# A gated linear attention with a rational feed-forward on one core: pairs of heads joined in one matmul step, fourteen joined polynomial steps, and another order of all steps

## The chip, the core and the metric

The kernel runs on one core of a Trainium2 chip. The core has five engines with queues of their own: TensorE (PE in the profile, with its weight loads as PEld), VectorE (DVE), ScalarE (ACT), GpSimd (POOL) and SyncE (SP, which here only issues transfers). Each engine executes its own instructions in the order in which the program lists them; between engines, semaphores make one wait for another. Transfers run on 16 DMA engines that all queues share. The metric is the device time of one execution in microseconds; the kernel before took 212.11 us as the median of 3 runs (211.64 to 213.5).

## The reference

Two stages. The first is a recurrence per batch (4) and head (8) over 768 positions, with head size 48; the second is a feed-forward layer on 3072 tokens of width 384 with 2048 hidden units and a rational function between its two products.

```python
f = 1.0 / (1.0 + np.exp(-f_logit))
for t in range(S):
    state = f[:, :, t, :, None] * state + einsum('bhd,bhde', k[:, :, t], v[:, :, t])
    y[:, :, t] = einsum('bhd,bhde->bhe', q[:, :, t], state)
...
h = x @ w_in
P = a[0] + a[1]*h + a[2]*h**2 + a[3]*h**3
Q = 1 + abs(b[0])*abs(h) + abs(b[1])*h**2
return (P / (Q + 1e-6)) @ w_out
```

## The kernel before

**Units.** The work is cut into 12 units of 256 tokens: 4 batches times 3 stretches of the sequence (units 0 to 3 are the first stretches, 8 to 11 the last ones, and a unit needs the state of the unit four before it). The 256 tokens are interleaved in two (i), and a unit has two blocks (j) of 128 tokens, each on 64 partitions. Eight heads make four pairs (a).

**Steps of the recurrence.** `ld` loads f, k, q (issued by SP) and v (issued by POOL). `ef` and `ls` (ACT) make the logarithm of the gate, `cs` (PE) sums it along time, `A` (ACT) exponentiates it, once for k (x=1) and once for q (x=0). `xa` (DVE or POOL, a `p` in the step) multiplies k and q with it. `T` transposes the result on PE, `Te` copies it out of PSUM (ACT with an `s`, else DVE). `sc` multiplies k and q into scores, for two pairs of heads at a time (g), `mk` (DVE) masks them. `yb` multiplies the masked scores with v, `yi` multiplies q with the state before the block. `vm` copies the columns of v that lie across a boundary. `ic` and `si` (PE) and `st` (DVE) make the next state. `ye` (ACT with `s`, else DVE) copies y to x, in bf16.

**The step `yb`** holds, for both i, four pieces of two heads, the pairs a0 to a1, and both j. Each matmul is a small one: 64 partitions in (the block j), 32 columns out (the pair a), 128 columns of scores. A matmul thus occupies one of eight tiles of the PE array, two row groups by four column groups. In the kernel before, every unit has two such steps, one for pairs 0 and 1 and one for pairs 2 and 3, of 32 matmuls each, with other steps between them in nine of the twelve units.

**Steps of the feed-forward.** `h` (PE) is the first product, four tiles of 128 hidden units at a time; `hy` (ACT) copies it out. Then follow on 8 or 16 hidden tiles at a time (2048 or 4096 columns): `sq` (DVE) or `sa` (ACT) the square, `ab` (DVE) the absolute value, `zd` (a transfer that adds, issued by POOL) or `zv` (DVE) the sum for Q, `rq` (ACT) the reciprocal, `p1` and `p2` (DVE, one multiply and one add by a scalar) the two halves of the polynomial, `pm` (DVE) a product, `ta` (a transfer that adds) or `tv` (DVE) their sum, and `gm` (DVE) P/Q. `o` (PE) is the second product, four hidden tiles of one block at a time; `oe` copies it out and `so` stores it. `tab` loads an activation table on ACT.

**What sets the order.** `ORDER` (lines 19 to 100) is a written list of all steps. The program takes them one by one (the loop at the end of the kernel function), so the list gives each engine's order of instructions and each queue's order of transfers. `@n` is the slot of PSUM (four slots of two banks) that a step fills: it waits until the earlier content of that slot has been read. `!m` sets a mark and `^m` holds a POOL step behind the marked one. Rings of buffers add waits too: there is one ring place for the transposed q and k (`T`) and one for the masked scores (`scm`), two for `A`, three for the loads, three for g and z, two for the square.

In the loop at the end, each step is made as
```python
made = steps[name](*(int(x.lstrip("@")) if x.lstrip("@").isdigit() else x for x in args))
```

Of the kernel before, what the change touches and what calls it, by code (L numbers as in the profile page):

```python
# [8 lines left out]
F32 = mybir.dt.float32  # L9
BF16 = mybir.dt.bfloat16  # L10
# [18 lines left out]
hy 0 8 12; fb; ld 4 f; yb 1 0 2 @3; hy 0 12 16; yb 1 2 4; xa 2 1; yi 1 1; ye 1 s; p1 0 8 16; T 2 @2  # L29
A 3 1; ab 0 8 16; h 1 12 16 @1; Te 2 s; sq 0 8 16; h 1 8 12 @3; p2 0 8 16; hy 1 12 16; pm 0 8 16 !m3; ld 3 q  # L30
ic 2 @0; hy 1 8 12; vm 2 ^m3; sc 2 1 @2; st 2 0; sc 2 0 @1; mk 2 1; ld 3 k; si 2 1; ef 5; h 0 0 4 @3; st 2 1
ls 5; ld 6 f; ab 1 8 16; h 0 4 8 @2; ef 4; tv 0 8 16 !m5; hy 0 0 4; ld 4 k; xa 3 0 2 4 p ^m5; h 1 4 8 @0
mk 2 0; ls 4; ld 4 q; ld 3 v ^m4; hy 0 4 8; h 1 0 4 @3; xa 3 1; ld 4 v; hy 1 4 8; xa 3 0 0 2; yb 2 0 2 @1
ld 7 f; zv 0 8 16; hy 1 0 4; T 3 @2; p1 0 0 8; ef 6; yi 2 1; yb 2 2 4; sq 1 0 8; Te 3 s; cs 4 @0; ld 8 f
ye 2 s; ab 1 0 8; sc 3 0 @3; cs 5 @2; A 4 0; ab 0 0 8 !m8; xa 4 0 2 4 p ^m8; mk 3 0; A 4 1; ic 3 @1; sa 1 8 16
h 2 8 12 @0; st 3 0; ld 5 k; sq 0 0 8; si 3 1; h 2 12 16 @3; hy 2 8 12; pm 0 0 8 !m7; zd 0 0 8; ld 5 q
xa 4 1 2 4 p ^m7; ls 6; sc 3 1 @0; st 3 1 !m6; A 5 1; ld 6 k; vm 3 ^m6; mk 3 1; h 2 4 8 @1; ld 5 v; hy 2 12 16
xa 4 1 0 2; ef 7; yi 3 1 @0; xa 4 0 0 2; yb 3 0 2; wo 12 16; p1 1 8 16; hy 2 4 8; T 4 @3; wo 8 12
pm 1 8 16 !m10; A 5 0; ic 4 @1; wo 4 8; xa 5 1 0 2 p ^m10; si 4 0; Te 4 s; yb 3 2 4; st 4 0 !m11; ye 3 !m9
# [69 lines left out]
def kernel(  # L109
# [135 lines left out]
    def const_z(i):  # L245
# [375 lines left out]
```

## Time and profile before

| | |
|---|---|
| median of 3 runs | 212.11 us |
| the profiled execution, its own time | 210.19 us |
| its span, first to last instruction | 208.5 us |
| granted TensorE clock, mean | 0.988 |
| PE busy | 191.0 us, 92% |
| DVE busy | 187.0 us, 90% |
| ACT busy | 186.1 us, 89% |
| POOL busy | 77.8 us, 37% |
| from HBM and to HBM | 25.17 MB and 4.72 MB |

The busy time of an engine is the time in which at least one of its instructions is under way; instructions of one engine overlap a little, so the time from one start to the next is shorter than a duration. The windows of the profile give busy time by stage, with the number of instructions behind an x. In the timeline, square brackets hold the idle time of the engine ahead of an instruction and what ended it. The chain of waits is followed back from the end.

### The profile page before, as it was taken

Reading aid. Unit: us, or ns where it says so; the run is one execution under the profiler, and the core shown is the slowest. Engines: PE = TensorE matmul, PEld = TensorE weight load, DVE = VectorE, ACT = ScalarE, POOL = GpSimd, SP = SyncE. Lnnn points to the kernel's source line nnn. Section 1 sums busy time; section 2 is a strip of 40 time slices with the busy share of each in tenths; the row PEclk is TensorE's granted clock in tenths of the full one; section 3 lists DMA queues with packets and bytes.
Section 4 is the critical chain, followed back from the end, with each engine's and each line's share of the span. In section 5 each row is a group of like instructions: output and inputs, shape, how many; then the busy total and the mean of one; then the engine's idle time right before and its main releaser. Section 6 shows DMA issues by size and latency. Waiting matters only on the chain.

```text
span 208.5 us, 6605 instructions
## 1 busy us (share of the span) xinstructions
PE 191.0 (92%) x2894; PEld 139.4 (67%) x2894; DVE 187.0 (90%) x235; ACT 186.1 (89%) x172; POOL 77.8 (37%) x99
## 2 busy tenths in 40 slices
PE   1297799989999999999999999999999999999991
PEld 1165487867767778766888677678766766776650
DVE  3378579999999999999999989999999999999970
ACT  4756389999999999999999999999999999999871
POOL 6060610516961535026151760641674433412000
PEclk9999699999999999999999999999999999999998
DMA  6999999799999499999999999899999999998955
GB/s 98 287 300 186 271 220 253 186 220 233 168 206 202 85 176 152 249 267 265 208 222 252 250 199 229 209 200 210 185 191 163 214 211 195 193 190 183 238 146 167
DMA packets 61820, 43.15 MB, mean 207 GB/s; under 512 B 51424, under 2 KB 56544, under 8 KB 61792
## 3 DMA queue, kind: packets, MB, share of 16 engines
q0 software_dynamic: 20528, 23.86, 69.3%
q1 hardware_dynamic: 41184, 18.78, 34.7%
q8 instruction: 22, 0.36, 0.6%
q10 hardware_dynamic: 80, 0.10, 0.2%
q14 instruction: 6, 0.05, 0.1%
HBM read 25.17 MB, written 4.72 MB: 143 GB/s over the span
## 4 chain that ended last, share of the span: by engine, by line
PE 75%; DVE 10%; DMA 6%; SPq 4%; issue 2%; ACT 1%; DVEq 0%
PE op L549 31%; PE hp L469 26%; PE y L389 6%; SPq L209 4%; PE cs L304 3%; DMA v<-in_v_dram 3%; PE tp L345 3%; PE sc L368 2%; DMA q<-in_q_dram 2%; DVE scm L376 2%; DVE g L528 2%; PE sv L434 2%; DVE state L459 1%; PE sv L444 1%; DVE qkp L331 1%
## 5 line engine op out<-in xcount | busy, mean ns | idle before, releaser
L549 PE MATMUL op<-w_out_sb,g 128*128 128x384 bf16 x384 | 68.6, 326 | 0.0
L469 PE MATMUL hp<-x,w_in_sb 128*128 128x256 bf16 x576 | 68.0, 273 | 0.3 <-DVE state L459 0.3
L469 PEld LDWEIGHTS <-w_in_sb 128*128 128x128 bf16 x576 | 55.4, 98 | 9.4 <-issue 0.7
L549 PEld LDWEIGHTS <-g 128*128 128x128 bf16 x384 | 35.8, 98 | 22.6 <-DVE g L540 0.4
L481 ACT CAST hy<-hp 128x1024 bf16<-128x1024 f32 x48 | 47.8, 1027 | 2.6 <-PE hp L469 2.3
L508 ACT ACTIVATE z<-z 128x4096 bf16<-128x4096 bf16 (+1 forms) x16 | 44.5, 2780 | 1.1 <-DVE z L499 1.1
L540 DVE TENSOR_TENSOR g<-g,z 128x2048 bf16<-128x2048 bf16 (+2 forms) x24 | 28.9, 1218 | 1.1 <-issue 0.6
L503 POOL DMA_DIRECT2D z<-h x20 | 20.6, 1077 | 24.7 <-ACT h L490 17.0
L528 DVE TENSOR_TENSOR g<-g,h 128x2048 bf16<-128x2048 bf16 (+1 forms) x21 | 28.8, 1373 | 0.1
L376 DVE TENSOR_TENSOR scm<-sc,mask 128x1024 bf16<-128x1024 f32 x24 | 28.8, 1216 | 0.0
L490 ACT ACTIVATE h<-hy 128x2048 bf16<-128x2048 bf16 (+1 forms) x13 | 26.8, 2073 | 0.0
L326 ACT ACTIVATE A<-cs 128x768 f32<-128x768 f32 (+3 forms) x26 | 19.0, 779 | 6.5 <-PE cs L312 6.5
L532 POOL DMA_DIRECT2D g<-hy x15 | 13.8, 943 | 28.3 <-DVE g L528 9.3
L304 PE MATMUL cs<-lsp,Ui 128*128 128x384 bf16 (+1 forms) x39 | 12.0, 371 | 10.1 <-ACT lsp L294 8.7
L518 DVE TENSOR_SCALAR g<-hy,a_sb 128x2048 bf16<-128x2048 bf16 (+1 forms) x23 | 18.9, 829 | 1.4 <-ACT hy L481 1.4
L331 POOL TENSOR_TENSOR qkp<-k,A 128x384 bf16<-128x384 f32 x11 | 11.0, 1025 | 23.6 <-DVE g L540 10.4
L523 DVE TENSOR_SCALAR hy<-hy,a_sb 128x2048 bf16<-128x2048 bf16 (+1 forms) x20 | 18.3, 915 | 0.4
L209 POOL DMA_DIRECT2D v<-in_v_dram x12 | 12.1, 1012 | 15.7 <-DVE qkp L331 8.3
L494 DVE TENSOR_SCALAR z<-hy 128x2048 uint16<-128x2048 uint16 (+1 forms) x21 | 15.8, 764 | 0.0
L459 DVE TENSOR_TENSOR state<-sv,A 128x384 bf16<-128x384 f32 x20 | 11.0, 552 | 4.5 <-PE sv L444 2.4
L389 PE MATMUL y<-scm,v 64*32 64x128 bf16 x384 | 14.0, 218 | 0.8 <-DVE scm L376 0.7
L331 POOL TENSOR_TENSOR qkp<-q,A 128x384 bf16<-128x384 f32 x10 | 10.0, 1010 | 11.5 <-ACT A L326 5.5
(70 smaller groups left out, 246.4 us busy)
## 6 DMA issues: line engine op xcount, KB each, us to landing
z<-h POOLq DMA_DIRECT2D x20, 512.0 KB, 7.5
g<-hy POOLq DMA_DIRECT2D x15, 512.0 KB, 7.8
f<-in_f_logit_dram SPq DMA_DIRECT2D x11, 384.0 KB, 5.8
k<-in_k_dram SPq DMA_DIRECT2D x11, 384.0 KB, 7.7
q<-in_q_dram SPq DMA_DIRECT2D x11, 384.0 KB, 7.8
v<-in_v_dram POOLq DMA_DIRECT2D x12, 192.0 KB, 7.7
out_dram<-f SPq DMA_DIRECT2D x12, 192.0 KB, 3.9
out_dram<-osb SPq DMA_DIRECT2D x10, 192.0 KB, 6.4
```

Source lines behind the costliest of these rows:

```text
L209: return eng.dma_start(out=s[what][:, hh].rearrange("p h i d -> p h (i d)"), in_=src[s["b"], hh, t0:t0 + NT, :].rearrange("h (p i) d -> p ...
L331: i = (nc.gpsimd if eng == "p" else nc.vector).tensor_mul(s["qk"][:, x, :, hh, 0:D], s["qk"[x]][:, hh].rearrange("p h i d -> p i h d"), s[ ...
L376: return nc.vector.tensor_mul(t, s["sc", g].rearrange("s r a i t -> s (r a) (i t)"), mb)
L389: nc.tensor.matmul(s["y"][32 * a:32 * a + 32, j, kk * C:kk * C + C].rearrange("e (i t) -> e i t", i=2), lhsT, rhs, start=(j, a) not in s[" ...
L469: nc.tensor.matmul(t[:, m - m0, :].rearrange("f (j t) -> f j t", j=UB), w_in_sb[:, kk, m * P:(m + 1) * P], s["x"][:, :, kk, :], start=(kk ...
L481: nc.scalar.copy(fl(big(s, "hy"), m0, m1), fl(s["hp", m0], 0, m1 - m0))
L490: return nc.scalar.activation(fl(big(s, "h2"), m0, m1), fl(big(s, "hy"), m0, m1), AF.Square)
L503: return nc.gpsimd.dma_start(out=fl(big(s, "z"), m0, m1), in_=fl(big(s, "h2"), m0, m1), accum_op=ALU.add)
L508: return nc.scalar.add_instruction(mybir.InstActivation(name=nc.get_next_instruction_name(), func=AF.Reciprocal, ins=[nc.scalar.lower_ap(f ...
L528: return nc.vector.tensor_mul(fl(big(s, "g"), m0, m1), fl(big(s, "g"), m0, m1), fl(big(s, "h2"), m0, m1))
L540: return nc.vector.tensor_mul(fl(big(s, "g"), m0, m1), fl(big(s, "g"), m0, m1), fl(big(s, "z"), m0, m1))
L549: nc.tensor.matmul(s["op", g][:, j, 0:DM], big(s, "g")[:, m, C * j:C * j + C], w_out_sb[:, m, :], start=(s["on", j] == 1), stop=(s["on", j ...
```

## The change

1. `yb` is called once per unit, for all four pairs (12 steps of 64 matmuls where there were 24 of 32). The function is the same; the four pairs are the inner loop, so that eight matmuls that follow one another go to the eight different tiles.
2. Seven more `p1` and two more `p2` cover 16 hidden tiles at once; with those that did so before, 14 of the two kinds are joined. Three more `gm` and two more `pm` are joined too.
3. Some work moves between engines: one half of a `sq` goes from DVE to ACT (as `sa`, of which two more are joined), two `ye` go from ACT to DVE, one `oe` of half a unit from ACT to DVE, and one half of a q product (`xa`) from DVE to POOL.
4. `T` can be cut (a `c` in the step): 64 transposes of 64 by 64 in place of 16 of 128 by 128, with another layout of the result. Units 7, 10 and 11 use it.
5. A new step `dm` multiplies zeros by zeros (two matmuls of 512 columns each, whose result nobody reads); it stands in the list twice. `cz 4` clears its operand.
6. The list has another order from the first step to the last, on all engines and queues.

The core of the diff (the list of steps is shown at its first and last lines):

```diff
-cu 1; cz 1; ld 0 f 2 4; ld 0 v; ab_ b s; cz 3; cz 0; ld 0 f 0 2; ci; ld 0 q 2 4; ld 1 f; cu 0; ld 0 k 0 2
-ef 0 2 4; ls 0 2 4; cm; ld 0 k 2 4; cz 2; fa; cs 0 2 4 @0; ef 0 0 2; ls 0 0 2; ld 0 q 0 2; cs 0 0 2 @1; ld 1 k
-A 0 1 0 2; A 0 1 2 4; A 0 0 2 4; A 0 0 0 2; fr; ld 2 f; ef 1; xa 0 1 2 4; ls 1; xa 0 0 2 4; vm 0 v; cs 1 @2
-xa 0 0 0 2; ld 1 q; xa 0 1 0 2 !m0; ld 1 v ^m0; ld 3 f; ic 0 @3; wi 2 8 16; A 1 1; wi 3 8 16; A 1 0
-T 0 0 2 @0; st 0 0; ld 2 q; ab_ a s; wi 1 8 16; xa 1 1 2 4; T 0 2 4 @1; wi 0 8 16; Te 0 0 2 s; sc 0 0 @2
-xa 1 0 0 2; Te 0 2 4 s; xa 1 0 2 4; ef 2; si 0 1; sc 0 1 @0; xa 1 1 0 2; st 0 1; T 1 @1; mk 0 0; ld 2 k
-mk 0 1; yb 0 0 2 @3; yi 0 1; Te 1; ef 3; yb 0 2 4; ic 1 @2; ls 2; st 1 0 !m1; sc 1 1 @0; ld 2 v ^m1; ye 0 s
-cs 2 @1; mk 1 1 !m4; ls 3; sc 1 0 @3; wi 0 0 8; A 2 0; si 1 1; ld 5 f; cs 3 @0; wi 3 0 8; st 1 1; A 2 1
-vm 1 v !m2; wi 2 0 8; mk 1 0; xa 2 0 0 2 p ^m2; A 3 0; h 0 8 12 @2; wi 1 0 8; xa 2 0 2 4; h 0 12 16 @1
...
-so 8 0 2; o 10 0 4 8; gm 11 12 16; o 10 0 0 4; rq 11 0 8; gm 11 8 12; o 11 1 12 16 @2; tv 11 0 8
-o 11 0 8 12 @1; oe 9 0 2 s; o 11 0 12 16; gm 11 0 4; oe 10 0 2 s; o 11 1 8 12; so 9 0 2; gm 11 4 8; o 11 0 0 4
-o 11 0 4 8; so 10 0 2; o 11 1 4 8; oe 11 0 1 s; o 11 1 0 4; so 11 0 1; oe 11 1 2 s; so 11 1 2
+cu 1; cz 0; ld 0 k 2 4; cu 0; ld 0 f 2 4; cz 3; ld 1 f; ci; ld 0 f 0 2; cm; ab_ b s; ld 0 v; cz 2; cz 1
+ld 0 q 0 2; ld 0 k 0 2; ld 0 q 2 4; ef 1; ef 0 2 4; ld 1 q; ls 0 2 4; ef 0 0 2; cs 0 2 4 @0; fa; ls 0 0 2
+ls 1; cs 0 0 2 @1; ld 1 k; vm 0 v; fr; cs 1 @2; A 0 1 2 4; A 0 1 0 2; A 0 0 0 2; xa 0 1 0 2; A 0 0 2 4; ld 2 f
+xa 0 1 2 4; A 1 0; xa 0 0 0 2 !m0; ld 1 v ^m0; T 0 0 2 @3; ld 3 f; ic 0 @1; wi 2 8 16; Te 0 0 2 s; wi 0 8 16
+A 1 1; ld 2 k; ab_ a s; st 0 0; wi 3 8 16; xa 0 0 2 4; wi 1 8 16; xa 1 0 2 4; T 0 2 4 @0; xa 1 1 0 2
+xa 1 0 0 2; sc 0 0 @3; Te 0 2 4 s; xa 1 1 2 4; ld 2 q; ef 2; si 0 1; cz 4; sc 0 1 @2; st 0 1; ls 2; T 1 @0
+mk 0 1; ef 3; mk 0 0; ls 3; yi 0 1 @1; ic 1 @2; Te 1 !m1; yb 0 0 4; ld 2 v ^m1; ye 0 s; st 1 0; sc 1 1 @3
+vm 1 v; si 1 1; mk 1 1; sc 1 0 @0; wi 3 0 8; cs 3 @1; ld 5 f; wi 2 0 8; mk 1 0; cs 2 @3; wi 0 0 8; A 3 1
+wi 1 0 8; st 1 1; h 0 8 12 @0; A 2 1; A 3 0; xa 2 1 0 2; h 0 12 16 @2; xa 2 1 2 4; A 2 0; ld 4 f; fb
+hy 0 8 12; yb 1 0 4 @1; hy 0 12 16; yi 1 1; xa 2 0; ic 2 @3; ye 1; sa 0 8 16; T 2 @0; st 2 0; h 1 8 12 @2
...
+o 10 0 4 8; gm 11 12 16; rq 11 0 8; so 8 0 2; o 10 0 0 4; p2 11 0 8; o 11 0 12 16 @0; gm 11 8 12
+o 11 1 12 16 @1; tv 11 0 8; oe 9 0 2 s; o 11 0 8 12; so 9 0 2; oe 10 0 2 s; o 11 1 8 12; gm 11 0 4; gm 11 4 8
+o 11 0 0 4; so 10 0 2; o 11 0 4 8; o 11 1 4 8; oe 11 0 1 v; o 11 1 0 4; so 11 0 1; oe 11 1 2 s; so 11 1 2
...
+    zz = consts.tile([P, 512], BF16, name="zz")
...
+        elif i == 4:
+            return nc.vector.memset(zz, 0.0)
...
     def T(n, *args):
-        s = unit(n)
-        a0, a1, sl = args if len(args) == 3 else (0, HP, args[0])
-        t = s["tp", a0] = slot(sl, [P, 2, 2, HP, P], BF16, "tp")
+        s = unit(n)
+        *ab, sl = [x for x in args if x != "c"]
+        a0, a1 = ab or (0, HP)
+        cut = "c" in args
+        t = s["tp", a0] = slot(sl, [P] + ([UB, 2, 2, HP, R] if cut else [2, 2, HP, P]), BF16, "tp")
         for x in (1, 0):
             for i in range(2):
                 for p in range(a0, a1):
-                    nc.tensor.transpose(t[:, x, i, p, :],
-                                        s["qk"][:, x, i, 2 * p:2 * p + 2, :].rearrange("t h d -> t (h d)"), ident)
+                    if cut:
+                        for j in range(UB):
+                            m = slice(R * j, R * j + R)
+                            for par in range(2):
+                                nc.tensor.transpose(t[E * par:E * par + E, j, x, i, p, :],
+                                                    s["qk"][m, x, i, 2 * p + par, :], ident[m, m])
+                    else:
+                        nc.tensor.transpose(t[:, x, i, p, :],
+                                            s["qk"][:, x, i, 2 * p:2 * p + 2, :].rearrange("t h d -> t (h d)"), ident)
...
+    def dm(i, sl):
+
+        t = slot(sl, [P, 2, 512], F32, "dm")
+        for b in range(2):
+            nc.tensor.matmul(t[:, b, :], zz[:, 0:P], zz, start=True, stop=True)
```

`Te`, `sc` and `yi` read the cut layout through a view with the block j outermost; their instructions keep their number and sizes.

More of the change, by code (lines that the diff above doesn't have):

```diff
@@ L30 @@
[L30 to L39, printed above, removed]
@@ new lines @@
+ld 11 q; ta 3 0 8; ab 5 0 8; sc 7 1 @2; hy 6 4 8; zd 4 0 8; ld 9 v; sq 5 8 16 !m21; h 6 12 16 @0
+xa 9 0 2 4 p ^m21; mk 7 1; h 6 8 12 @3; tab 1; rq 3 0 8; p2 4 0 8; yi 7 0 @2; yi 7 1; zv 4 8 16; yb 7 0 4
+ta 4 0 8; ic 8; ye 7 s; ta 4 8 16; ld 10 v ^m19; st 8 0; hy 6 12 16; tv 3 8 16; h 7 4 8 @2; zd 5 0 8
+hy 6 8 12; p1 5 0 16; T 8 @1; rq 3 8 16; h 7 0 4 @0; pm 5 8 16; ld 10 k; Te 8 s; h 7 8 12 @3; gm 3 0 8
+hy 7 4 8; vm 8 v; cs 10 @1; gm 3 8 16; hy 7 0 4; o 3 0 4 8 @2; pm 5 0 8; hy 7 8 12; o 3 0 12 16; rq 4 0 16
@@ L352, in Te @@
         s["T"] = ring["T"][n % len(ring["T"])]
-        dst, src = (t[:, :, :, a0:a1].rearrange("p x i a t -> p (x i) (a t)") for t in (s["T"], s["tp", a0]))
+        if len(s["tp", a0].shape) == 6:
+            s["T"] = s["T"].rearrange("p x i a (j t) -> p (x i a j t)", j=UB).rearrange(
+                "p (j x i a t) -> p j x i a t", j=UB, x=2, i=2, a=HP)
+            dst, src = (t[:, :, :, :, a0:a1].rearrange("p j x i a t -> p (j x i) (a t)") for t in (s["T"], s["tp", a0]))
+            s["Tj"] = [s["T"][:, j] for j in range(UB)]
+        else:
+            dst, src = (t[:, :, :, a0:a1].rearrange("p x i a t -> p (x i) (a t)") for t in (s["T"], s["tp", a0]))
+            s["Tj"] = [s["T"][:, :, :, :, R * j:R * j + R] for j in range(UB)]
         if "s" in args:
@@ L402, in yi @@
             for a in range(HP):
-                ymm(s, j, a, kk, state(s, j)[:, a, 32 * kk:32 * kk + 32], s["T"][:, 0, :, a, R * j:R * j + R])
+                ymm(s, j, a, kk, state(s, j)[:, a, 32 * kk:32 * kk + 32], s["Tj"][j][:, 0, :, a, :])
     def yb(n, a0=0, a1=HP, sl=None):
```

121 lines of the change are left out of this document (61 added, 60 removed).

## The prediction

> **What bounds the kernel now.** I read the page first, for the balance of the engines, then three windows of it.
>
> ```profile
> PE 191.0 (92%) x2894; PEld 139.4 (67%) x2894; DVE 187.0 (90%) x235; ACT 186.1 (89%) x172; POOL 77.8 (37%) x99
> PE   1297799989999999999999999999999999999991
> DVE  3378579999999999999999989999999999999970
> ACT  4756389999999999999999999999999999999871
> ```
>
> ```profile
> 0.00:30.00 30.00, 18.66 (x372) 14.22 (x373) 17.30 (x50) 17.48 (x26) 10.51 (x24) 0.94 1.12 226
> 30.00:200.00 170.00, 168.21 (x2502) 122.93 (x2500) 167.93 (x184) 166.15 (x144) 67.29 (x75) 1.00 1.06 207
> 200.00:208.50 8.50, 4.14 (x26) 2.25 (x24) 1.74 (x3) 2.43 (x5) 0.00 (x0) 0.90 0.50 139
> ```
>
> The columns after the length are the busy times of PE, PEld, DVE, ACT and POOL, then the clock and the DMA. From 30 to 200 us three engines are full at once: DVE is idle for 170 - 167.93 = 2.07 us, ACT for 3.85, PE for 1.79. What is lost lies ahead of 30 us (DVE 12.7, ACT 12.5) and behind 200. So a faster PE alone would gain nothing that DVE and ACT do not also give. Now the chain of waits (start, length, what), for PE's own rates.
>
> ```profile
> 109.31 1.68 PE y L389 x88
> ...
> 115.02 0.89 PE tp L345 x16
> 115.91 2.60 PE op L549 x16
> ...
> 123.38 1.33 PE hp L469 x12
> 124.71 1.27 PE y L389 x88
> ...
> 158.26 0.56 PE y L389 x32
> ...
> 185.91 18.24 PE op L549 x112
> ```
>
> The last row is PE at work without a gap up to 204.15 us. The other two engines end just ahead of it (timeline):
>
> ```profile
> 198.14 1.91 ACT L508 ACTIVATE z<-z 128x2048 bf16<-128x2048 bf16 x1 [1.06 <-DVE z L499]
> 200.55 1.29 DVE L540 TENSOR_TENSOR g<-g,z 128x1024 bf16<-128x1024 bf16 x2
> ```
>
> The last `gm` ends at 201.84, and PE works 2.31 us more. Behind it, in both lists, stand 12 `o` matmuls whose cost is 2.60 / 16 = 0.163, 1.95 us. So DVE has 0.36 us of slack at the end; all three engines are the bound.
>
> **The change on DVE.** Groups of instructions, with mean ns after the busy time:
>
> ```profile
> L518 DVE TENSOR_SCALAR g<-hy,a_sb 128x2048 bf16<-128x2048 bf16 x22 | 17.6, 805 | 1.4 <-ACT hy L481 1.4
> L518 DVE TENSOR_SCALAR g<-hy,a_sb 128x4096 bf16<-128x4096 bf16 x1 | 1.3, 1343 | 0.0
> L523 DVE TENSOR_SCALAR hy<-hy,a_sb 128x2048 bf16<-128x2048 bf16 x16 | 12.9, 809 | 0.3
> L523 DVE TENSOR_SCALAR hy<-hy,a_sb 128x4096 bf16<-128x4096 bf16 x4 | 5.4, 1338 | 0.1
> L540 DVE TENSOR_TENSOR g<-g,z 128x2048 bf16<-128x2048 bf16 x18 | 21.7, 1216 | 0.3 <-ACT z L508 0.2
> L540 DVE TENSOR_TENSOR g<-g,z 128x4096 bf16<-128x4096 bf16 x2 | 4.6, 2288 | 0.6 <-issue 0.6
> L485 DVE TENSOR_TENSOR h<-hy 128x2048 bf16<-128x2048 bf16 x10 | 12.2, 1220 | 0.0
> L454 DVE TENSOR_SCALAR x<-y,sig 128x768 bf16<-128x768 f32 x2 | 2.0, 1013 | 0.0
> L331 DVE TENSOR_TENSOR qkp<-q,A 128x384 bf16<-128x384 f32 x12 | 6.5, 551 | 0.4 <-DMA q<-in_q_dram 0.4
> ```
>
> Seven more joined `p1` save 7 x (2 x 0.805 - 1.343) = 1.87; two `p2` 2 x (2 x 0.809 - 1.338) = 0.56; three `gm` 0.43; two `pm`, taken at the rows of `gm`, 0.29. One `sq` that goes saves 1.22, one half `xa` 0.55; two `ye` cost 2.03. Together -2.89 by durations. But starts lie closer than durations say:
>
> ```profile
> 29.86 0.81 DVE L518 TENSOR_SCALAR g<-hy,a_sb 128x2048 bf16<-128x2048 bf16 x1 [1.40 <-ACT hy L481]
> 30.59 0.69 DVE L494 TENSOR_SCALAR z<-hy 128x2048 uint16<-128x2048 uint16 x1
> ```
>
> The next one starts 0.73 us after the first, so 0.08 of each instruction is covered by its neighbour. 14 instructions fewer lose 14 x 0.08 = 1.12 of that cover: **DVE -1.8 us**. The `oe` on DVE comes behind the last `gm`, where DVE is free. `cz 4` falls into the start.
>
> **On ACT.** Its rows:
>
> ```profile
> L490 ACT ACTIVATE h<-hy 128x2048 bf16<-128x2048 bf16 x12 | 23.1, 1940 | 0.0
> L490 ACT ACTIVATE h<-hy 128x4096 bf16<-128x4096 bf16 x1 | 3.7, 3658 | 0.0
> L452 ACT ACTIVATE x<-y 128x768 bf16<-128x768 f32 x10 | 8.1, 809 | 2.5 <-PE y L389 2.4
> ```
>
> `sa` goes from 12 halves and 1 whole to 9 and 3: +1.49. Two `ye` go: -1.62. With three instructions fewer, at the same overlap, **ACT +0.1 us**. Of its 3.85 us of idle time after 30 us most waits for PE (`hy`, `ye`) or for `zv` at the end; with PE ahead I let 1.5 us of it go, between 0 and 3.85.
>
> **On PE.** A unit with two separate `yb` takes 1.68 us with its `yi` (88 matmuls); one in which the two stood together (unit 8) 1.27. How eight tiles run is seen there, in PE's timeline:
>
> ```profile
> 124.93 0.33 PE L389 MATMUL y<-scm,vmp 64*32 64x128 bf16 x16
> 125.04 0.33 PE L389 MATMUL y<-scm,v 64*32 64x128 bf16 x12
> ```
>
> While the two halves ran into each other, 16 matmuls started in 0.11 us, 6.9 ns each. A half alone has four tiles, and its row of 32 is 0.56 us, 17.5 ns each. I take a joined `yb` at 64 x 6.9 ns plus 0.12 for filling and draining (an estimate), 0.56 us; the other bound is two halves' worth, 1.12, no gain. In nine units that saves 0.56; in the three where the halves stood together, which are 1.68 - 1.27 = 0.41 shorter already, 0.15. Together 5.5 us, some 4 of them in the full stretch. A cut `T` has 64 matmuls in four tiles: between 0.44 and 1.12 us (the same two rates) against 0.89, near 0.6 I think, since its moving side has 64 columns and not 128; three save 0.9 (between 1.3 saved and 0.7 lost). A `dm` costs two matmuls of 512 columns, by the slope between `hp` (256 columns, 0.111) and `op` (384, 0.163) 0.215 each: 0.43 twice, the first in the start, where PE idles. So **PE -4.5 us** in the full stretch (from +1 to -6), more than the others give, and PE stops being the tightest. What that costs: a joined `yb` waits for the second `mk` of its unit, and all of PE's queue behind it.
>
> ```profile
> L376 DVE TENSOR_TENSOR scm<-sc,mask 128x1024 bf16<-128x1024 f32 x24 | 28.8, 1216 | 0.0
> ```
>
> In the new list at least 3 us of `h` and `o` stand between the last `sc` and the `yb` of each unit from 2 on (unit 7: two `h` at 1.33 and two `yi`; unit 11: two `o` at 0.65, one `h`, two `yi`), against one `mk` of 1.22 or two. I count the wait as nothing; without that cover it is up to 1.2 us a unit.
>
> **The start.** Rows of PE, DVE and ACT, then the chain:
>
> ```profile
> 3.42 0.52 ACT L289 ACTIVATE f<-f 128x384 f32<-128x384 f32 x1 [1.32 <-DMA f<-in_f_logit_dram]
> 10.05 0.56 DVE L331 TENSOR_TENSOR qkp<-k,A 128x384 bf16<-128x384 f32 x1 [3.42 <-DMA k<-in_k_dram]
> 22.19 0.32 PE L304 MATMUL cs<-lsp,Ui 128*128 128x384 bf16 x1 [1.36 <-issue]
> 24.66 0.56 DVE L459 TENSOR_TENSOR state<-sv,A 128x384 bf16<-128x384 f32 x1 [2.45 <-PE sv L444]
> 26.14 2.65 PE hp L469 x24
> ```
>
> ```profile
> GB/s 98 287 300 186 271 220 253 186 220 233 168 206 202 85 176 152 249 267 265 208 222 252 250 199 229 209 200 210 185 191 163 214 211 195 193 190 183 238 146 167
> ```
>
> Before, f comes first and k last: ACT begins at 3.42, DVE then waits 3.42 us for k. After, SP issues half of k, half of f, all of f of unit 1 and only then the other half of f, and ACT's first step is `ef 1`. That needs 768 KB; at 98 to 287 GB/s (5.2 us slices) some 4 us, so ACT begins near 5.7, 2.3 us later. In return `ls 1` is done ahead of the first `A`, k is there when `A` is, and `xa` begins near 10.5 (5.7, then two whole and four half steps and two `A`, at the 0.52 of a half), half a microsecond later than before. POOL issues v behind the constants and not between them; `ic` needs it only after `xa`, which I count as time enough. POOL also gets one more half `xa` over the whole kernel, at a share of 37%: nothing. Then the new list has `sc 1 0` ahead of both `cs` of units 2 and 3. Before, PE sat 1.36 us for nothing that the profile shows, then did a `cs`, and `sc 1 0` came after it: the 2.45 us of DVE. With `mk 1 0` right behind `mk 1 1` these go, and `cs`, `A`, `h` and `hy` follow earlier. Against it: `st 0 0` (0.56) and its wait for `ic` ahead of the last `xa` of unit 0, and `cz 4`. I take **-2.0 us** for the start, for DVE as for ACT; the ends are -3.9 (the waits of 2.45 and 1.40 both gone) and +2.3 (ACT's late beginning never made good).
>
> **The sum.** DVE: -1.8 - 2.0 - 0.3 of end slack = -4.1. ACT: +0.1 - 2.0 - 1.5 = -3.4. PE: -4.5 and its earlier start. The smallest gain decides, ACT's, -3.4, shortened to -3.3 for the `dm` in mid-stretch: span 205.2, with the 1.69 us around it 206.9 against 210.19. The median stands 1.92 above that execution, so it should come to 212.11 - 3.3 = **208.8 us**, 1.6% faster. About 1% is what a measurement of this kernel tells from no change.
>
> **Rivals.** (a) The three engines interlock as before but the start gains nothing, because the late f costs ACT what the earlier `sc` gives: -1.5, 210.6. For it: the 768 KB ahead of the first ACT step. Against: DVE's 3.42 us of waiting for k is room for it.
>
> (b) The joined `yb` does not do what it says, the eight tiles running no faster than four: PE stays the bound at its old work plus 0.43 and up to 0.7, only the start is gained: -1, 211. Against it: the 16 matmuls in 0.11 us.
>
> (c) Slower: PE's instructions do not arrive in time. Instructions too are fetched by DMA:
>
> ```profile
> q8 instruction: 22, 0.36, 0.6%
> ```
>
> That is 16 KB a packet. The gap of 1.36 us came after 223 matmuls and as many weight loads, at a place where no engine was late. The change uses up instructions faster: 128 in 0.56 us for a `yb`, and the three cut `T` add 288. If such a gap opens at six of the twelve units, 8.2 us are lost against 3.3 gained: 217. It decides against the change from four gaps on (5.4 - 3.3 = 2.1, 1%). Against it: the full stretch of before has no such gap, though 88 matmuls pass in 1.27 us there.
>
> [...]
>
> (d) ACT's and DVE's idle time goes wholly as PE runs ahead: -6, 206.
>
> **Chances.** Forecast (207.3 to 210) 0.49, (d) 0.11: faster by over 1% 0.60. (a) 0.16 and (b) 0.07: within 1%, 0.23. (c), with `yb` held by late masks as its smaller kin, 0.17. The range runs from (d), with the most that the start gives, 204.6, up through (a) and (b) to the first part of (c), 214.0.
>
> **What would show it.** Joined `yb` rows of 64 near 0.56 us; DVE busy near 184.5 and ACT near 186; the first `h` near 24.5 us and not 26; no gap of PE named "issue" over 1 us; more PE idle time than 1.79 us between 30 us and the end. It is wrong if PE shows gaps between 60 and 180 us, or if `xa` of unit 0 begins after 12 us.

## The result, and the profile after

The changed kernel takes 212.36 us (median of 12 runs, 210.24 to 213.23), the kernel before beside it 210.34 us (12 runs, 208.09 to 213.5): a ratio of 1.013, 95% interval 1.0089 to 1.017. It is 1.3% slower, where 1.6% faster was forecast. The profiled execution of the changed kernel took 210.24 us and is the fastest of its twelve; that of before, 210.19 us, is near the middle of its own. So the two profiles show what the change did at its best, and not what it costs in most executions. Ratios leave out executions over 1.5% slower than the fastest of the same kernel, medians keep them; the kernel with only `yb` joined, below, has no ratio, since four of its six were such.

The profile's page of the changed kernel, then its busy times in the same three windows as before (length, PE, PEld, DVE, ACT, POOL, clock, DMA):

```profile
PE 188.6 (90%) x3042; PEld 135.6 (65%) x3042; DVE 188.7 (90%) x223; ACT 186.0 (89%) x168; POOL 80.7 (39%) x100
...
q8 instruction: 24, 0.39, 0.7%
```

```profile
0.00:30.00 30.00, 19.56 (x394) 14.66 (x395) 18.84 (x52) 18.70 (x27) 9.49 (x23) 1.00 1.10 215
30.00:200.00 170.00, 164.93 (x2629) 118.81 (x2627) 167.44 (x169) 166.03 (x140) 71.18 (x77) 1.00 1.07 209
200.00:209.00 9.00, 4.16 (x25) 2.09 (x23) 2.38 (x4) 1.30 (x3) 0.00 (x0) 0.99 0.50 133
```

TensorE did 3.3 us less in the full stretch and now idles 5.07 us there; VectorE and ScalarE idle 2.56 and 3.97 us, as before (2.07 and 3.85). VectorE has 12 instructions fewer and 1.7 us more busy time. The chain of waits shows the joined `yb`, the cut `T`, and TensorE twice without work that it waited for:

```profile
21.46 0.14 DVE vmp L400
21.60 0.86 issue
22.46 0.34 PE sv L461
...
27.67 0.61 PE y L406 x58
28.29 0.29 issue
28.58 0.53 PE y L406 x18
...
76.64 0.67 PE y L406 x64
97.33 0.64 PE tp L352 x64
125.68 1.11 PE y L406 x88
```

A joined `yb` takes 0.67 us (forecast 0.56, two halves 1.12), with its `yi` 1.11 where it was 1.68 or 1.27; a cut `T` 0.64 against 0.89.

Now VectorE and GpSimd side by side, in the timeline (start, length, what). Line 546 is `p2`, 393 `mk`, 471 `ye`, 559 `tv`, 331 `xa`:

```profile
49.00 1.22 DVE L393 TENSOR_TENSOR scm<-sc,mask 128x1024 bf16<-128x1024 f32 x1
50.13 1.39 DVE L546 TENSOR_SCALAR hy<-hy,a_sb 128x2048 bf16<-128x2048 bf16 x1
51.45 1.41 DVE L541 TENSOR_SCALAR g<-hy,a_sb 128x4096 bf16<-128x4096 bf16 x1
52.77 1.00 DVE L471 TENSOR_SCALAR x<-y,sig 128x768 bf16<-128x768 f32 x1
53.70 1.53 DVE L559 TENSOR_TENSOR g<-g,hy 128x2048 bf16<-128x2048 bf16 x1
...
111.14 1.45 DVE L546 TENSOR_SCALAR hy<-hy,a_sb 128x2048 bf16<-128x2048 bf16 x1
```

```profile
49.28 1.40 POOL L331 TENSOR_TENSOR qkp<-k,A 128x384 bf16<-128x384 f32 x1
...
52.99 1.14 POOL L331 TENSOR_TENSOR qkp<-k,A 128x384 bf16<-128x384 f32 x1
...
110.54 1.49 POOL L331 TENSOR_TENSOR qkp<-q,A 128x384 bf16<-128x384 f32 x1
```

A half `p2` took 0.809 us before; these two take 1.39 and 1.45, and the `tv` 1.53 where its like take 1.22. Each began while a GpSimd product was still under way. `mk` and `ye` beside the same products keep their 1.22 and 1.00. Seven VectorE instructions are longer than the shortest of their shape by over 0.1 us (0.15 to 0.65 each), 2.7 us together; all seven lie beside GpSimd's products, its copies (`vm`) or its transfer issues. Before, none is: nearly the whole of each GpSimd product lies beside a `mk`, `ye` or `st` (18.2 of 21.4 us beside `mk` alone). One of them, GpSimd's product and VectorE's `mk`, before:

```profile
49.62 0.99 POOL L331 TENSOR_TENSOR qkp<-k,A 128x384 bf16<-128x384 f32 x1 [0.25 <-ACT lsp L294]
49.77 1.21 DVE L376 TENSOR_TENSOR scm<-sc,mask 128x1024 bf16<-128x1024 f32 x1
```

The start, ScalarE, VectorE and TensorE:

```profile
6.38 1.25 ACT L289 ACTIVATE f<-f 128x768 f32<-128x768 f32 x2 [4.29 <-DMA f<-in_f_logit_dram]
...
10.98 1.03 DVE L331 TENSOR_TENSOR qkp<-k,A 128x384 bf16<-128x384 f32 x2 [0.51 <-DMA k<-in_k_dram]
...
24.89 2.78 PE L492 MATMUL hp<-x,w_in_sb 128*128 128x256 bf16 x24
```

The first `h` begins at 24.89 us against 26.14, and VectorE had done 1.54 us more by 30 us. The last `gm` ends at 201.93 us against 201.84: all of the lead is gone.

### The profile page after: what moved, and what is told of

Same layout as the page of the kernel before. It is cut to its first block, busy times and chain, and to the rows that moved or that the text cites. A ratio compares the mean times of both kernels' runs of the same rounds, so it can differ in the third digit from the quotient of the medians.

```text
span 208.5 us, 6879 instructions
## 1 busy us (share of the span) xinstructions
PE 188.6 (90%) x3042; PEld 135.6 (65%) x3042; DVE 188.7 (90%) x223; ACT 186.0 (89%) x168; POOL 80.7 (39%) x100
## 4 chain that ended last, share of the span: by engine, by line
PE 51%; DVE 23%; ACT 12%; issue 7%; DMA 3%; SPq 2%; DVEq 0%; ACTq 0%
PE op L572 22%; PE hp L492 17%; ACT hy L504 5%; PE y L406 4%; DVE scm L393 4%; DVE g L563 3%; DMA k<-in_k_dram 3%; DVE hy L546 3%; DVE g L541 2%; PE sc L385 2%; DVE g L551 2%; DVE qkp L331 2%; DVE g L559 2%; PE cs L304 2%; DVE state L476 2%
## 5 line engine op out<-in xcount | busy, mean ns | idle before, releaser
L572 PE MATMUL op<-w_out_sb,g 128*128 128x384 bf16 x384 | 69.8, 327 | 1.5 <-ACT A L326 0.8
L531 ACT ACTIVATE z<-z 128x2048 bf16<-128x2048 bf16 (+1 forms) x16 | 44.5, 2778 | 0.6 <-DVE z L522 0.6
L526 POOL DMA_DIRECT2D z<-h x20 | 21.8, 1128 | 23.0 <-ACT h L513 18.9
L513 ACT ACTIVATE h<-hy 128x2048 bf16<-128x2048 bf16 (+1 forms) x12 | 28.2, 2348 | 0.0
L326 ACT ACTIVATE A<-cs 128x784 f32<-128x784 f32 (+3 forms) x26 | 18.8, 772 | 2.4 <-PE cs L312 2.3
L304 PE MATMUL cs<-lsp,Ui 128*128 128x384 bf16 (+1 forms) x39 | 11.1, 344 | 8.5 <-ACT lsp L294 8.2
L207 POOL DMA_DIRECT2D v<-in_v_dram x12 | 13.3, 1107 | 14.2 <-DVE qkp L331 8.6
L331 POOL TENSOR_TENSOR qkp<-q,A 128x384 bf16<-128x384 f32 x11 | 11.5, 1047 | 7.2 <-DVE qkp L331 4.0
L289 ACT ACTIVATE f<-f 128x768 f32<-128x768 f32 (+1 forms) x13 | 10.0, 799 | 4.3 <-DMA f<-in_f_logit_dram 4.3
L372 ACT COPY T<-tp 128x1024 f32<-128x1024 f32 (+1 forms) x12 | 11.4, 954 | 1.9 <-PE tp L355 1.9
```

Of the source, the lines that this page charges most:

```text
L331: i = (nc.gpsimd if eng == "p" else nc.vector).tensor_mul(s["qk"][:, x, :, hh, 0:D], s["qk"[x]][:, hh].rearrange("p h i d -> p i h d"), s[ ...
L513: return nc.scalar.activation(fl(big(s, "h2"), m0, m1), fl(big(s, "hy"), m0, m1), AF.Square)
L526: return nc.gpsimd.dma_start(out=fl(big(s, "z"), m0, m1), in_=fl(big(s, "h2"), m0, m1), accum_op=ALU.add)
L531: return nc.scalar.add_instruction(mybir.InstActivation(name=nc.get_next_instruction_name(), func=AF.Reciprocal, ins=[nc.scalar.lower_ap(f ...
L572: nc.tensor.matmul(s["op", g][:, j, 0:DM], big(s, "g")[:, m, C * j:C * j + C], w_out_sb[:, m, :], start=(s["on", j] == 1), stop=(s["on", j ...
```

## The experiments

Theory A: GpSimd lengthens VectorE's steps where the new order puts them beside each other. Theory B, called the page theory in the expectations: TensorE's instructions come in blocks of 256 (counted under B), here called instruction pages (not the pages of the profile), and the new order uses them up faster than they come. Rivals: the joined steps themselves cost something; the new order is slower for its waits. All ratios are against the kernel before on the same chip, whose median there lay between 209.67 and 210.65 us; the groups of runs were on different chips, so ratios tell more than medians.

| kernel | median, us | ratio, 95% interval |
|---|---|---|
| changed, again | 211.74 | 1.0132, 1.0061 to 1.0202 |
| changed, `yb` in halves | 212.2 | 1.0111, 1.0051 to 1.0171 |
| changed, `p1`, `p2` in halves | 213.47 | 1.0235, 1.0161 to 1.031 |
| before, `yb` joined | 214.7 | none |
| before, `p1`, `p2` joined | 212.41 | 1.012, 1.0049 to 1.0192 |
| changed, three moves (A) | 211.65 | 1.0062, 1.0018 to 1.0106 |
| changed, 48 idle matmuls | 215.61 | 1.0229, 1.0119 to 1.034 |
| changed, 128 idle matmuls | 213.75 | 1.0188, 1.0114 to 1.0261 |
| before, 64 idle matmuls | 210.26 | 1.0016, 0.9985 to 1.0048 |
| before, `yb` and `p` joined | 211.85 | 1.0113, 1.0063 to 1.0164 |
| the same, 64 idle matmuls | 210.94 | 1.0012, 0.9962 to 1.0062 |
| before, `yb` joined, 64 idle | 212.67 | 1.01, 1.0045 to 1.0154 |
| moves, 48 idle, 80 idle at 66 us | 214.55 | 1.0229, 1.0171 to 1.0288 |
| moves, v of unit 2 early | 212.46 | 1.0131, 1.0073 to 1.0189 |
| moves, 48 idle, 80 idle at 85 us | 212.32 | 1.0136, 1.0077 to 1.0196 |
| the same, v of unit 2 early | 212.92 | 1.0132, 1.0045 to 1.0218 |
| changed, 48 idle, `T 7` whole | 211.41 | 1.0041, 0.9993 to 1.0089 |
| moves, 48 idle, `T 7` whole | 210.72 | 0.9999, 0.9951 to 1.0047 |

One execution of `changed, 48 idle, T 7 whole` took 466.33 us; why is open.

### Parts alone

```diff
-yb 0 0 4
+yb 0 0 2; yb 0 2 4
```
(and so for all 12, in the changed order)

> The changed kernel with each joined step of scores and v written as two halves again, side by side at the same place. Theory that VectorE and its collisions with GpSimd bound the changed kernel: no change beyond 1 us, since PE has idle time there (4 us between 30 and 190 us). Rival that the joined step costs time through the fetch of instructions: faster by 1 to 2 us.

```diff
-p1 1 0 16
+p1 1 0 8; p1 1 8 16
```
(and so for the 14 joined `p1` and `p2`, in the changed order)

> The changed kernel with the 14 joined p1 and p2 as two halves each, side by side at the same place. By starts, 14 joins save 14 x 0.20 us, so if VectorE bounds the changed kernel this is slower by 2 to 3 us. If what stretches the joined ones (1.41, 1.73 and 1.80 us against 1.34) hits a long instruction more than two short ones, it is slower by less than 1.5 us. If another engine bounds it, less than 1 us either way.

> The changed kernel once more, for another trace of it and the granted clock of each execution. The profiled execution had a span of 208.5 us at a mean clock of 1.0, the others 209.4 to 211.5 at 0.973 to 0.998. If windows of half clock early in the span make the difference, an execution at 0.98 shows one or two windows of 3.4 us at 0.5, behind a stretch in which PE idles, and steps of PE in them take twice as long. If not, its later stages are longer at full clock.

```diff
-yb 0 0 2; ...; yb 0 2 4
+yb 0 0 4
```
(and so for all 12, in the order before)

> The kernel before with one edit: the two half steps of products of scores and v of each unit are one step for all four pairs, at the place of the second half. If the joined step does what it says (64 matmuls in about 0.6 us in place of 2 x 0.56) and PE was the tightest engine of before, this is faster than before by 1 to 4 us. If VectorE and ScalarE are as tight as PE, it gains less than 1 us although PE's busy time falls by 2 to 5 us. If the joined step itself is what costs the changed kernel its time, this is slower than before by about 2 us.

Halving `yb` again moves the changed kernel by less than the intervals tell. With `yb` joined in the order before, two executions took 208.55 and 210.97 us against a median of 209.67, and four took 214 to 216.4 for a reason that stays open. So joined `yb` does what it says (0.67 us), and no run here shows it to be worth anything by itself. Halving the `p` steps costs 1.0% of the time (the intervals overlap at their ends), and VectorE shows it in the profile's page:

```profile
PE 188.8 (89%) x3040; PEld 135.5 (64%) x3042; DVE 191.0 (90%) x237; ACT 186.5 (88%) x168; POOL 79.8 (38%) x100
```

188.7 to 191.0 us busy: the joined `p` steps help by about 2 us and are not what makes the kernel slower. That the time follows VectorE here fits VectorE as the bound of the changed order.

### A: GpSimd beside VectorE

```diff
-ld 5 v; cs 5 @2; xa 4 0 0 2; ...; xa 4 0 2 4 !m5; xa 4 1 2 4 p ^m5
+cs 5 @2; xa 4 0 0 2 !m5; ...; xa 4 0 2 4; xa 4 1 2 4 p ^m5; ld 5 v
-ld 9 v; sq 5 8 16 !m21; ...; xa 9 0 2 4 p ^m21
+sq 5 8 16 !m21; ...; xa 9 0 2 4 p ^m21; ld 9 v
```

> The changed kernel with three small moves in the list: the fetches of v for units 5 and 9 come behind the GpSimd products they stood ahead of, and one GpSimd product of unit 4 is released one VectorE step earlier. Nothing else differs. Theory that GpSimd's products lengthen VectorE's bf16 steps beside them: the two p2 that took 1.39 and 1.45 us in the changed kernel take 0.81 each, VectorE's busy time falls from 188.7 to near 187.4, and the time falls by about 1.2 us. Rival, that VectorE's lengthening is hidden by other waits: the two p2 shrink but the time stays within 0.4 us of the changed kernel's. Second rival, that they are long for a reason of their own: they stay at 1.4.

VectorE and GpSimd of this kernel near the second place (lines moved up by one):

```profile
111.45 1.22 DVE L392 TENSOR_TENSOR scm<-sc,mask 128x1024 bf16<-128x1024 f32 x1
112.58 0.80 DVE L545 TENSOR_SCALAR hy<-hy,a_sb 128x2048 bf16<-128x2048 bf16 x1
```

```profile
111.67 1.00 POOL L330 TENSOR_TENSOR qkp<-q,A 128x384 bf16<-128x384 f32 x1 [0.16 <-issue]
```

The product now begins 0.22 us into the `mk` and ends 0.09 us into the `p2`: 0.80 us in place of 1.45. At the first place the `p2` only fell to 1.20, since the issue of v took the product's place beside it. VectorE's busy time is 187.6 us (188.7 before the moves, 187.4 expected), and the time 211.65: about half of the loss is back, though the two intervals overlap. That GpSimd lengthens these steps is shown; its price in time is shown only together with B, below. Five steps of VectorE still are too long with the moves, by 1.5 us together.

### B: pages of TensorE's instructions

In the trace's record of DMA packets (queue q8), TensorE's instructions arrive in packets of 16 KB, 22 before and 24 after, for 2894 and 3042 matmuls with as many weight loads: counted by where the packets begin, one for 256 instructions, 127 or 128 matmuls with their weight loads. The gap near 22 us came in every unshifted kernel after matmul 223, though the steps there differ (`cs 2` before, `si 1 1` after); TensorE went on 1.42 us after the end of a packet before, 1.31 after. In these two profiles a packet began only once the boundary ahead had been passed, at once or up to 4.7 us later, while other transfers ran. At the first boundary it began 3.9 (before) and 3.3 us (after) behind it and had landed after 4.8 and 4.2. So an instruction page used up in less than about 5.5 us, an estimate (the 4.2 to the landing and the 1.31 behind it, after), can leave TensorE without instructions; it need not, since some of 5.1 and 5.2 us in the kernel before, whose next packet came sooner, left no gap.

```diff
+cz 4; dx 48 64 @3
 cu 1; cz 0; ld 0 k 2 4; cu 0; ...
...
+    def dx(k, cols, sl):
+        t = slot(sl, [P, 2, 512], F32, "dm")
+        for b in range(k):
+            nc.tensor.matmul(t[0:32, 0, 0:cols], zz[:, 0:32], zz[:, 0:cols], start=True, stop=True)
```

> The changed kernel with 48 idle matmuls (zeros, 64 columns) on TensorE in the first microseconds, before it has anything to do, so that every later instruction of TensorE stands 96 places further on; the clearing of the zeros moves to the start. Theory that TensorE's instructions come in pages of 256 (about 127 matmuls with their loads), each asked for when the page before is entered and ready some 5.6 us later: from the changed kernel's own start times, matmuls 1577 and 2341 of the old count come 2.1 and 3.6 us after the previous boundary, so TensorE stands still for about 3.5 and 2.0 us there, with smaller gaps near 2086 and 2851; 6 us of gaps in all, and the time is 3 to 6 us longer. The first stall moves from matmul 223 to the old number 175. Rival, that the gaps of the start are waits of another kind and the pages are hidden: no new gap above 1 us, and the time within 1 us of the changed kernel's.

> The control: the same with 128 idle matmuls (8 columns), 256 instructions, one whole page. Page theory: every boundary falls where it fell in the changed kernel, so there is no new gap between 30 us and the end, and the time is within 1 us of the changed kernel's (less, if a warm TensorE helps the start). Rival, that more instructions of TensorE or a busy start cost something in themselves: it is slower by as much as the version with 48.

TensorE's timeline with the 48, at the old place of the gap (line 460, `si 1 1`) and at the two new ones:

```profile
21.40 0.32 PE L460 MATMUL sv<-state,ident 128*128 128x384 bf16 x1
...
101.17 0.26 PE L405 MATMUL y<-scm,v 64*32 64x128 bf16 x5
102.57 0.23 PE L405 MATMUL y<-scm,v 64*32 64x128 bf16 x3 [1.14 <-issue]
...
146.41 0.94 PE L497 MATMUL hp<-x,w_in_sb 128*128 128x256 bf16 x7
149.04 1.14 PE L497 MATMUL hp<-x,w_in_sb 128*128 128x256 bf16 x9 [1.69 <-issue]
```

The gap at 22 us is gone. Two open in the middle of a `yb` and of an `h`, after matmuls 1627 and 2395, where with the 48 the instruction pages had been reckoned to end after 1625 and 2389; each ends 1.3 us after a packet. They are smaller than the 3.5 and 2.0 us reckoned, and the smaller ones did not show; the ratio is 1.0% over the changed kernel's, with overlapping intervals, and the median 3.2 us. With 128, a whole instruction page, there is no gap by issue over 0.4 us behind 30 us, and the first one stands at the same step again, now 2.4 us long (TensorE's waits):

```profile
PE sv L460 <- issue: 2.4, 1, 2.4
```

It was the control in place, not in cost: this kernel was 1.4 us slower than the changed one, 0.4 more than allowed, with the granted clock at half from 23.0 to 29.9 us behind that gap.

> The kernel before, in its own order, with 64 idle matmuls (zeros, 8 columns) on TensorE in the first microseconds; every later TensorE instruction stands 128 places, half a page, further on. Page theory, from the start times of the kernel before: with this shift only one page boundary comes less than 5.4 us after the one ahead of it (by 0.6 us), where unshifted the first boundary costs 1.4 to 1.9 us and three later ones come too early by 1.6 us together. The gap of TensorE named issue near 22 us goes, and the time falls by 1 to 2 us, to about 208.5: faster than both kernels. Rival, that what follows that gap in the start is set by transfers and VectorE anyway: the gap goes and the time stays within 0.5 us of 210.2.

> The kernel before, in its own order, with all 12 yb joined and 13 pairs of p1 or p2 halves joined; no shift. Theory that TensorE, VectorE and ScalarE bound together and that instruction pages add to it: TensorE loses 5 us of work and VectorE 2, but with joined yb three early boundaries cost up to 2.6 us, so the time lies within 1 us of 210.2. Rival, that the three engines alone decide (pages hidden): 2 us faster than before. Second rival, that the places of the joined halves delay their consumers: slower, as with the p joined alone (1.2%).

> The same with the 64 idle matmuls at the start. Page theory: the first gap goes, and the early boundaries of the joined yb shrink from 2.6 us to 0.2, so this is 2 to 4 us faster than the same without the shift, about 207 to 208. Rival, pages hidden: the same time as without the shift, within 0.7 us.

> The kernel before in its own order, with 13 pairs of p1 or p2 halves joined in the place of one of the two. Theory that VectorE bounds: 13 joins at 0.27 us by durations less 0.08 of lost overlap each are 2.4 us; VectorE busy falls from 187.0 to near 184.5 and the time by 1.5 to 2.4 us, so this is faster than both kernels. Rival, that TensorE bounds the kernel before (75% of its chain of waits was TensorE's): less than 0.7 us is gained and TensorE's share of the chain stays above 70%.

```diff
+cz 4; dx 64 8 @3
 cu 1; cz 1; ld 0 f 2 4; ld 0 v; ...
...
-p1 3 8 16; ...; p1 3 0 8
+p1 3 0 16
```
(in the two without `yb` joined or without idle matmuls only one of these edits; 13 `p` pairs. In the three with `p` joined, the joined `p1` of unit 9 overwrites values that the last `o` of unit 6 then reads, and in the one with `p` alone |h| of half of unit 2 is taken behind its `p2`; number and sizes of instructions are as they should be.)

In the order before, the gap at 22 us went as expected and nothing was gained (1.0016): the rival holds there. With `yb` and `p` joined the shift took 1.0% off (1.0113 without, 1.0012 with it; the intervals lie just beside each other), as B expected in direction, but it gave 0.9 us by medians and not 2 to 4, and level with before is where it ended. The `p` joined alone brought VectorE down and the time up, which neither of its two expectations had:

```profile
PE 192.1 (91%) x2894; PEld 139.4 (66%) x2894; DVE 185.2 (88%) x222; ACT 186.4 (88%) x172; POOL 81.1 (38%) x99
```

```profile
30.00:200.00 170.00, 166.59 (x2518) 121.49 (x2509) 163.68 (x168) 165.04 (x143) 70.56 (x75) 1.00 1.05 203
```

VectorE then idles 6.3 us in the full stretch and TensorE 3.4 against 1.8. The likely reason, argued and not shown: many joined steps stand later than the first half did, and what they feed waits.

> The kernel before in its own order with all yb joined and 64 idle matmuls at the start. Page theory: joined yb alone came to nothing because early page boundaries (2.6 us by its start times) took what they saved; shifted, only 0.2 us is left, TensorE shows over 4 us more idle time, and VectorE and ScalarE bound: 0.3 to 1.5 us faster than the kernel before. Rival, that VectorE and ScalarE were as tight as TensorE: no difference over 0.3 us.

This was a miss. The time was 1.0% over before's. In its profile the `gm` of units 0 to 10 end 0.6 to 1.3 us earlier than before, and the last one 0.04 later: VectorE at the end waits for a transfer (its waits from 30 to 202 us):

```profile
DVE g L546 <- DMA g<-hy: 1.0, 1, 1.0
```

### Pages and the start together

```diff
 o 0 0 8 12 @2
+dy 0 80
```
(80 idle matmuls of 8 columns, beside 48 at the start and the three moves; the version at 85 us has `dy 1 80` behind `o 1 0 4 8` instead)

> The changed kernel with the three moves that spare VectorE, 48 idle matmuls at the start and 80 more behind the first o (near 66 us), so that from there on the page boundaries fall where they fell, one page later. Page theory: the first gap of TensorE (1.1 to 2.4 us near 21 us) goes, as it did with the 48 alone, and the gaps of 1.1 and 1.7 us that the 48 alone had at matmuls 1627 and 2395 do not appear; against the same without idle matmuls (211.65 us) the time falls by 1 to 2 us, less the 1 us of the 80 matmuls as far as TensorE bounds there. Rival, that the gap in the start is absorbed behind it: within 0.5 us of 211.65.

> The changed kernel with the three moves that spare VectorE, and the fetch of v of unit 2 no longer held behind the copy of unit 1. Theory that the wait of TensorE for that v (0.6 to 3.1 us near 28 to 30 us in the runs) is what eats a start that gets ahead: the wait goes; alone it gains 0 to 0.7 us on 211.65, since in this order the first gap of TensorE comes ahead of it and delays everything anyway. Rival, that an earlier v only delays w_in, f and k on the shared transfers: up to 1 us slower.

```diff
-Te 1 !m1; yb 0 0 4; ld 2 v ^m1
+Te 1; yb 0 0 4; ld 2 v
```

> The changed kernel with the three moves, 48 idle matmuls at the start and 80 more behind the first o of unit 1 (near 81 us), where 127 matmuls take 12 us, so that no page is used up early; v of unit 2 held as in the changed kernel. Page theory: no gap named issue over 0.5 us behind 30 us, no gap near 21 us; but TensorE waits 1.5 to 3 us for v near 29 us. So the time is 0 to 1 us less than 211.65. Rival, that idle matmuls cost as such: 1 to 3 us slower, as in the version with 80 of them near 66 us.

> Both: pages moved and v of unit 2 not held. Page theory with v as what was late next: neither gap nor wait in the start, the granted clock stays full there, and the time is 1.5 to 2.5 us less than 211.65, at 209 to 210, level with the kernel before or a little ahead of it. Rival, that the changed order is slower for reasons that lie behind the start: no less than 211 although the first h starts before 24.5 us.

With the 48 alone TensorE had waited 1.6 us for v of unit 2 at 28 us, so the fetch of v was tried too. All four missed. The 80 idle matmuls at 66 us used most of an instruction page up by themselves (80 of its 127 or 128 matmuls), and a gap of 2.0 us followed. At 85 us they did not, but held TensorE themselves, and ScalarE behind it (timelines of the version with v held):

```profile
84.78 2.16 PE L497 MATMUL op<-zz 128*32 128x8 bf16 x80
```

```profile
94.00 0.81 ACT L594 ACTIVATE osb<-op 128x768 f32<-128x768 f32 x1 [1.99 <-PE op L584]
```

The `gm` of unit 2, whose input ScalarE had made before that wait, still ended 1.02 us ahead of the version with the moves alone (91.63 against 92.65). An early v gained nothing.

```diff
+cz 4; dx 48 64 @3
...
-T 7 c @3
+T 7 @3
```
(the idle matmuls here have 8 columns; an uncut `T` has 48 matmuls fewer, so the instruction pages lie as in the changed kernel behind it)

> The changed kernel with the three moves that spare VectorE, 48 idle matmuls at the start, and T of unit 7 not cut: its 16 transposes in place of 64 take the 48 places back, so that behind it every page boundary falls where it fell in the changed kernel, with no idle matmul in the full stretch. From the start times of the version with the moves alone, no boundary then comes less than 5.2 us after the one ahead. Page theory: no gap named issue over 0.5 us anywhere, and the lead of 1.2 us that the version with 48 and 80 idle matmuls had at the last gm of unit 2 (91.55 against 92.71 us) is kept to the end: 210.4 by the median against 211.65, level with the kernel before. Rival, that the order loses it again behind the start for other reasons: 211.5 or more, with the lead gone before 120 us though TensorE shows no gap by issue.

> The changed kernel with the 48 idle matmuls at the start and T of unit 7 not cut, without the three moves. Page theory with VectorE's lengthened steps as a second, separate loss: the first gap goes here too, the time is about 1.2 us less than the changed kernel's 212.36 and 0.7 to 1.2 us more than the version that has the moves as well. Rival, that only one of the two decides: the same time as the version with the moves, or the same as the changed kernel.

Both times came near what the page theory expected. With the moves: 0.9999 (0.9951 to 1.0047), the loss is gone. Without them: 1.0041. The profile's page of the one with the moves, and its full stretch:

```profile
PE 189.0 (91%) x3042; PEld 136.0 (65%) x3042; DVE 187.7 (90%) x223; ACT 186.0 (89%) x168; POOL 80.5 (39%) x100
```

```profile
30.00:200.00 170.00, 165.62 (x2603) 119.94 (x2597) 166.74 (x168) 166.38 (x141) 71.01 (x77) 1.00 1.06 209
```

TensorE shows no gap by issue over 0.35 us in either. The last `gm` ends 1.13 us ahead of the version with the moves alone (201.65 against 202.78); at the `gm` of unit 2 it was 0.63, half of the lead expected. The other half arose at the next `gm`, and the trace shows where. TensorE with the moves alone, then with the instruction pages moved too (`T 7`, then the `cs` that follows):

```profile
98.30 0.71 PE L351 MATMUL tp<-ident,qkp 64*64 64x64 bf16 x64
105.64 0.32 PE L303 MATMUL cs<-lsp,Ui 128*128 128x384 bf16 x1 [0.58 <-ACT lsp L293]
```

```profile
97.57 1.06 PE L354 MATMUL tp<-ident,qkp 128*128 128x128 bf16 x16
104.50 0.34 PE L303 MATMUL cs<-lsp,Ui 128*128 128x384 bf16 x1
```

The whole `T 7` alone costs TensorE time (16 transposes in 1.06 us against 64 in 0.71). The wait of 0.58 us, which the profile puts down to ScalarE, ends 1.26 us after a packet of TensorE's instructions, behind matmul 1627; behind the gaps called issue TensorE went on as long after a packet. In the other version that packet came 4.1 us earlier and the wait is gone. In the profile of the changed kernel it is 0.18 us.

So A and B mended together take the 1.3% away: the interval of that version lies wholly under that of the changed kernel. The share of each is not settled, since the intervals of neighbours overlap. A rival is that what helps is the clearing of the zeros (`cz 4`), which moved to the start too, or a TensorE at work there; the version with 128 idle matmuls has both with every boundary in place, and was not faster than the changed kernel (1.0188). No version beat the kernel before.

## Why the prediction was wrong

**TensorE, -4.5 us: right in kind.** The `yb` was put at 0.56 us and took 0.67, the cut `T` at 0.6 and took 0.64; TensorE did 3.3 us less in the full stretch and stopped being the tightest. Rival (b) is out.

**VectorE, -1.8 us: this step failed.** Its durations were right: the instructions alone, at the shortest time of their shape and without `cz 4` and the `oe` behind the last `gm`, come to 2.75 us less (2.89 reckoned), and 1.0 us of overlap was lost (1.12 reckoned). What was left out is GpSimd. "POOL also gets one more half xa over the whole kernel, at a share of 37%: nothing" counted a share of time where the place counts; the same sum of products, put beside other steps, went with 2.7 us of lengthening on VectorE. Up to the last `gm` VectorE was busy 188.66 - 0.56 = 188.1 us against 186.97: +1.1 and not -1.8. In the version with A and B mended it is 187.15, still 0.2 more than before, with 1.6 us of overlap lost; so the forecast gain does not come there either. The trace shows the lengthening step by step: the `p2` at 50.13 is 0.59 us longer than the shortest of its shape (1.39 against 0.80), and the product beside it ends 0.55 us after its start; the `mk` beside the same product keeps its 1.22. Why the two products beside the `p2` took 1.40 and 1.49 us, where one beside a `mk` takes 1.00, is open, and so is what lengthens a step beside a product: no run here shows it.

**The start, -2.0 us: half right, then lost.** In the profiled execution VectorE was 1.54 us ahead at 30 us (ScalarE 1.2), with ScalarE's first step at 6.38 and not 5.7, `xa` at 10.98 and not 10.5, the first `h` at 24.89 and not 24.5. Sum for VectorE: +1.1 - 1.5 and 0.5 more idle in the full stretch is +0.1, which is what the last `gm` shows (201.93 against 201.84). In the other executions part of the lead in the start is lost too, as the next paragraph tells.

**From one execution to the median.** The forecast added the gap that the kernel before had between its profile and three runs. With 12 runs that gap shrank from 1.92 to 0.15 us, and for the changed kernel it was 2.12. In the second profile of the changed kernel the first gap was 1.1 us, a second one, in the middle of `yb 1`, 0.6, and every `gm`, from the first on, ended 0.8 us later; the granted clock was at half from 17.0 to 20.4 us. That execution took 211.01 us; what the ones of 212 and more lost beyond it was not profiled. The granted clock points to the same: in 16 executions of the changed kernel 0.984 in the mean against 0.995 in the 68 of before that the ratios of the experiments use; where it was 0.994 or more, the changed kernel took 210.72 us in the mean (3 of 16) and before 209.32 (46 of 68), below that 212.47 and 210.59. With the instruction pages moved and the moves made, the mean is 0.991.

**Rival (c): real, mainly at another place.** TensorE's instructions do not always arrive in time, but in the profile of the changed kernel no gap over 0.4 us of that kind opened between 60 and 180 us (0.18 us at 104, and 0.58 there in the version with the moves); the condition "four gaps in the stretch" was not met, and by its start times the order uses up no instruction page there in under 5.6 us. Most of what is seen is in the start, where the gap of before stayed and a second one came. "No gap of PE named issue over 1 us" held in the profile by 0.14 us and failed in others. Moving every instruction by 96 places moved the gaps with the instruction pages: the one at 22 us closed, and two of 1.14 and 1.69 us opened behind matmuls 1627 and 2395, where pages had been reckoned to end. Moving them by 256 brought the first back at its step. So here the measurement decides for (c) as to the cause, though not as to the place.

**ScalarE, +0.1 and 1.5 us of idle time to go:** its sum of -3.4 set the forecast. Its busy time was right (186.0), but of the 2.0 us of the start 1.2 came, and no idle time went (3.85 before, 3.97 after); 1.8 us of it still were waits of `hy` for TensorE. With VectorE at +0.1 in place of -4.1, VectorE and not ScalarE decided.

## What to carry to other kernels

Where two engines get in each other's way, look at what stands beside what, not at shares: here `mk` and `ye` kept their 1.22 and 1.00 us beside GpSimd's products, while seven bf16 steps of VectorE beside its products, copies or issues took 0.15 to 0.65 us more. In an order written out by hand, count TensorE's instructions too: they came here in blocks of 256, the packet that began behind the first boundary had landed 4.8 (before) and 4.2 us (after) after it, and 48 idle matmuls at the start closed a gap at 22 us and opened two of 1.14 and 1.69 us behind 100 us. Before a sum is made on one profiled execution, see where that execution stands among many.

## What the hardware showed unexpectedly

- Packets of TensorE's instructions began up to 4.7 us after the boundary ahead was passed and took 0.88 to 1.44 us (profiles of before and after); where TensorE stood still for one it went on 1.42 (before) and 1.31 us (after) after its end. Instruction pages used up in 5.6 us or more mostly left no gap; two that were reckoned at 2.1 and 3.6 us, with the 48 idle matmuls, left 1.14 and 1.69.
- The granted clock was at half in stretches of 3.41 us (22.49 to 25.91 us before, 17.0 to 20.4 in the second profile of the changed kernel) or of twice that (23.0 to 29.9 us with 128 idle matmuls). Between 40 and 200 us this was seen twice, each time within 3 us of a gap of TensorE of 1.6 and 2.0 us (before with `yb` and `p` joined; 80 idle matmuls at 66 us); but a gap of 1.69 us at 147 us was not followed by one. In the start it came in 12 of 19 profiles (mean clock up to 30 us 0.77 to 0.94 there, 1.00 in the others), in changing places. What decides there is open.
- An idle matmul of 32 weights by 8 columns took 27 ns (80 in 2.16 us), more than the 10.5 ns of a real one of 128 columns in eight tiles (64 in 0.67 us).
